# Two more Strassen products taken to a second level in the last down projection

## The chip, the cores and the metric

The kernel runs on one core of one Trainium2 chip. The metric is the device time of one execution, in microseconds (us). Five engines run their own instruction streams: TensorE (PE) multiplies and PEld loads its stationary operand, VectorE (DVE), ScalarE (ACT) and GpSimd (POOL) work on tiles, and SyncE (SP) issues nearly all transfers. Intermediate sums of the matrix products lie in eight PSUM banks; everything else lies in on-chip tiles or in memory.

## The reference

The reference is a linear-attention block followed by a gated feed-forward block, both with a layer norm in front and a residual added behind, on 2048 tokens of width 1024, with an inner width of 3584:

```python
def _B_ref(x, W_gate, W_up, W_down):
    gate = jnp.einsum("bsd,df->bsf", x, W_gate)
    up = jnp.einsum("bsd,df->bsf", x, W_up)
    gate = gate * (gate > 0)
    h = gate * up
    return jnp.einsum("bsf,fd->bsd", h, W_down)

h = x + _A_ref(_layernorm(x), A_wqkv, A_wo)
h2 = h + _B_ref(_layernorm(h), B_W_gate, B_W_up, B_W_down)
```

All inputs are bfloat16. The change touches the feed-forward block alone.

## The kernel before

The tokens of the feed-forward block are done in two passes of 1024. Each pass has a gate/up part of 14 *pairs* (two blocks of 128 inner columns a pair, `strassen_pair`, L1316) and a down part (`down_pass`, L1420). The attention block runs ahead of the first pass.

The order of work is written out by hand. Python builds one list of operations per engine (`_Plan`, L45 to 130). Each engine runs its list strictly in order, and waits are derived from which buffers an operation reads and writes. So the place in the program decides what is queued behind a waiting operation. This holds for SyncE too, whose list holds the transfers.

**Down part.** The output of a pass has 1024 tokens by 1024 columns. It is cut into 2 x 2 blocks of 512 tokens by 512 columns, and computed with Strassen's seven products (Winograd's form), numbered 0 to 6 in order of time. For each product the activations (or sums of them: D1 to D4) are multiplied by a block of W_down or by a sum of blocks (`t_scr`, made in the first gate/up pass by `wd_sums`, L650, and stored in memory). Products alternate between banks 0 to 3 (`XB`) and 4 to 7 (`YB`).

- A *direct* product (`direct`, L1547) has 56 matmuls of 512 columns, and takes its weights in five chunks (`WCH`).
- A *second-level* product (`level2`, L1575) applies the same scheme once more inside the product. It has seven steps, M1, M7, M6, M2, M5, M4 and M3 in this order, each of 14 matmuls of 256 columns with one weight chunk of 448 KB. The steps share four banks. ScalarE copies a bank to the next twice (`dfk`), and VectorE adds a bank into its target after M7 (two adds), M2, M5, M4 and M3. Step M3 accumulates into the bank that the add after M5 reads, so M3 waits for that add.

Before the change, products 1, 3, 5 and 6 are second-level and 0, 2 and 4 direct, in both passes. Each second-level product needs four sums of activations (`l2_sums`, L1509: VectorE, 1792 elements per partition, both operands in on-chip memory) and four sums of weights (`wl_sums`, L666, made in the first gate/up pass and stored in `l_scr`).

The products end in sums with each other and with the residual tiles: `U` starts as a copy of product 0, `V` is U plus product 3, and so on. The residual of the block (token half, column half) is fetched from `h_scr` in four tiles (`ld_h`, L1424) into a ring of eight slots, and GpSimd adds it to U or V (`add_h`, L1476), or makes the output of block (1,1) from `dsum` (`p_22`, L1469). VectorE makes the other outputs. `at(product, unit, ...)` hangs operations behind a unit of the list: a step of a second-level product, or a chunk of a direct one. Outputs are issued when `st_flush` is reached.

**Weight chunks.** `load_wd_next` (L612) issues the next chunk in order, each time a chunk was used, into the slot that came free. The first pass has a ring of 7 slots and the second of 13, of which six are gate/up weight slots (`RWG`) that the last three pairs leave:

```python
X_AT = [(NPAIR - 3) * 2 + i for i in range(NWX)]
RING = [[NWS - 2, NWS - 1] + list(range(NWS - 2))]
RING.append([RING[0][(len(WLIST) + i) % NWS] for i in range(NWS)] +
            [NWS + (NPAIR * 2 + x) % NWG for x in X_AT])
```

In the profile, L718 is every matmul, L723 every ScalarE copy, L543 every transfer and L1434 every sum of the down part: these are lines of helpers, so groups are told apart by tiles (`ps` is PSUM).

Of the kernel before, what the change touches and what calls it, by code (L numbers as in the profile page):

```python
# [132 lines left out]
def bass_sequential_preLN__linear_attn_block__glu_gated_reglu__prompt_kernel(  # L133
# [66 lines left out]
    l_scr = nc.dram_tensor("l_scr", [(len(L2O) + 1) * 4 * P, WDW], f16).ap()  # L200
# [5 lines left out]
    with es:  # L206
# [16 lines left out]
        NWX = 6  # L223
# [37 lines left out]
        hnT = RH[:].rearrange("p (a b) -> p a b", a=NDC)  # L261

# [42 lines left out]
        wdring += [RWG[:, i * NDC * 2 * P:i * NDC * 2 * P + WDW] for i in range(NWG)]  # L305
# [44 lines left out]
        def bank(b, w=512):  # L350
            return ps[:, b, 0:w]
# [22 lines left out]
        sl_lw = slots("dlw_", 2)  # L374
        sl_out = slots("dout_", NOS)
# [56 lines left out]
        B_out2 = bufs("out2_", STB)  # L432
        B_wd = bufs("wd_", NWS + NWX)
# [50 lines left out]
        for i in range(NWX):  # L484
            B_wd[NWS + i].over = [B_w[i]]
# [108 lines left out]
        WSRC = [("b", 0, 0), ("l", 1), ("b", 1, 0), ("l", 2), ("t", 0), ("l", 3), ("l", 4)]  # L594
        LSRC = [("q", 0, 0), ("s", 2), ("s", 1), ("q", 1, 0), ("s", 0), ("s", 3), ("q", 1, 1)]
        WLIST = []
        for src in WSRC:
            if src[0] == "l":
                WLIST += [("l", src[1]) + x for x in LSRC]
            else:  # L600
                WLIST += [src + c for c in WCH]

        X_AT = [(NPAIR - 3) * 2 + i for i in range(NWX)]
        RING = [[NWS - 2, NWS - 1] + list(range(NWS - 2))]
        RING.append([RING[0][(len(WLIST) + i) % NWS] for i in range(NWS)] +
                    [NWS + (NPAIR * 2 + x) % NWG for x in X_AT])

        def wd_slot(L):
            r = RING[L // len(WLIST)]
            return r[L % len(WLIST) % len(r)]  # L610

        def load_wd_next():  # L612
            L = wd_next[0]
            if L >= NPASS * len(WLIST):
                return
            wd_next[0] += 1
            i = wd_slot(L)
            src = WLIST[L % len(WLIST)]
            dst = wdring[i]
            if src[0] != "b":  # L620
                dst = dst.bitcast(f16)
            if src[0] == "l":
                dst = dst[:, 0:WDW].rearrange("p (m c) -> p m c", c=HNW)
                o = src[1]
                if src[2] == "q" and o == 4:
                    k, h = src[3:]
                    dma(sl_wd[i], wdring[i].rearrange("p (m c) -> p m c", c=HNW),
                        wd_v[:, 1, k:NPAIR:2, NW + h * HNW:NW + (h + 1) * HNW], "ld_wr_%d" % L, writes=[B_wd[i]])
                elif src[2] == "q":
                    k, h = src[3:]  # L630
                    dma(sl_wd[i], dst, t_v[:, o, k:NPAIR:2, h * HNW:(h + 1) * HNW], "ld_wq_%d" % L, reads=B_tscr,
                        writes=[B_wd[i]])
                else:
                    dma(sl_wd[i], dst, l_v[:, o - 1, src[3]], "ld_wl_%d" % L, reads=B_wscr if o == 4 else B_lscr,
                        writes=[B_wd[i]])
                return
            q0, q1 = src[-2:]
            dst = dst[:, 0:(q1 - q0) * NW].rearrange("p (q c) -> p q c", c=NW)
            if src[0] == "b":
                dma(sl_wd[i], dst, wd_v[:, src[1], q0:q1, src[2] * NW:(src[2] + 1) * NW], "ld_wd_%d" % L,  # L640
                    writes=[B_wd[i]])
            else:
                dma(sl_wd[i], dst, t_v[:, src[1], q0:q1, :], "ld_wt_%d" % L, reads=B_tscr[q0:q1],
                    writes=[B_wd[i]])
# [763 lines left out]
        os_ctr = [0]  # L1408
        wd_use = [0]
        U_ = [ftmp[:, j, :] for j in range(STB)]  # L1410
        V_ = [ftmp[:, STB + j, :] for j in range(STB)]

# [4 lines left out]
        X0v = hh16[:, 0:NFT:2, 0:SBW]  # L1417
        X1v = hh16[:, 0:NFT:2, SBW:2 * SBW]

        def down_pass(ps_, fill):  # L1420
            XB, YB = [0, 1, 2, 3], [4, 5, 6, 7]
            hr = {}

# [25 lines left out]
            def put(blk, dh, j, in0, in1, reads, eng="dve"):  # L1449
                k = os_ctr[0] % NOS  # L1450
                os_ctr[0] += 1
                tt(outst[:, k, :], in0, in1, reads, [B_outst[k]], "out_%d_%d_%d" % (blk, j, dh), eng=eng)
                st_out(blk, dh, j, sl_out[k], outst[:, k, :], B_outst[k])
# [5 lines left out]
            def e_s1(j):  # L1459
                ident_act(U_[j], bank(XB[j]), [B_bank[XB[j]]], [B_U[j]], "ds1")  # L1460

# [4 lines left out]
            def e_22(j):  # L1466
                tt(dsum[:, j, :], bank(XB[j]), V_[j], [B_bank[XB[j]], B_V[j]], [B_dsum[j]], "d22")

            def p_22(j):  # L1469
                h, hb = hv(1, 1, j)  # L1470
                put(1, 1, j, dsum[:, j, :], h, [B_dsum[j], hb], "pool")

            def e_u5(j):
                tt(U_[j], bank(XB[j]), U_[j], [B_bank[XB[j]]], [B_U[j]], "dU5")

            def add_h(dst, bufs_, blk, dh, j):  # L1476
                h, hb = hv(blk, dh, j)
                tt(dst[j], dst[j], h, [hb], [bufs_[j]], "dh", eng="pool")

            def quad(base, T, H):  # L1480
                return ftmp[:, base + 2 * T:base + 2 * T + 2, H * HNW:(H + 1) * HNW]
# [4 lines left out]
            def l2_add(dst, bd, src, bs, T, H, b, name):  # L1486
                tt(quad(dst, T, H), qb(b), quad(src, T, H), [B_bank[b]] + ([] if src == dst else bs[2 * T:2 * T + 2]),
                   bd[2 * T:2 * T + 2], name)

            def l2_out(ost, bo, base, bs, T, H, b):  # L1490
                tt(ost[:, 2 * T:2 * T + 2, H * HNW:(H + 1) * HNW], qb(b), quad(base, T, H),
                   [B_bank[b]] + bs[2 * T:2 * T + 2], bo[2 * T:2 * T + 2], "out_%d%d" % (T, H))

            def a_hh(k, t, f=hh):
                return (lambda q, j: f[:, 2 * q + k, (t * STB + j) * P:(t * STB + j + 1) * P]), \
                       (lambda q: B_hh[2 * q + k][t])
# [4 lines left out]
            def d2(q):  # L1501
                tt(D2[:, q, :], D1[:, q, :], hh[:, 2 * q, 0:SBW], [B_D1[q], B_hh[2 * q][0]], [B_D2],
                   "D2_%d" % q, op=ALU.subtract)

            def d4(q):
                tt(hh16[:, 2 * q + 1, 0:SBW], hh[:, 2 * q + 1, 0:SBW], D2[:, q, :], [B_D2],
                   [B_hh[2 * q + 1][0]], "D4_%d" % q, op=ALU.subtract)

            def l2_sums(quarter, dst, name):  # L1509
                def go(j, x, y, op):  # L1510
                    d, bd = dst(j)
                    tt(d, x[0], y[0], x[1] + y[1], bd, "%s_%d" % (name, j), op=op)
                Q = quarter
                return [
                    lambda: go(2, Q(0, 0), Q(0, 1), ALU.subtract),
                    lambda: go(0, Q(0, 1), Q(1, 1), ALU.add),
                    lambda: go(1, dst(0), Q(0, 0), ALU.subtract),
                    lambda: go(3, Q(1, 0), dst(1), ALU.subtract),
                ]

            def q_d2(k, t):
                return D2[:, k:NPAIR:2, t * SHB:(t + 1) * SHB], [B_D2]

            def q_hh(par, f):
                def go(k, t):
                    i0 = 2 * k + par
                    return f[:, i0:NFT:4, SBW + t * SHB:SBW + (t + 1) * SHB], [B_hh[i][1] for i in range(i0, NFT, 4)]
                return go

            def sg_ro(j):  # L1530
                return sg_o[:, j], [B_sgo[j]]

            def sg_x0(j):
                b0, c0 = NM * (j // 2), (j % 2) * SHB
                return X0v[:, b0:b0 + NM, c0:c0 + SHB], [B_hh[2 * (b0 + m)][0] for m in range(NM)]

            def sg_x1(j):
                b0, c0 = NM * (j // 2), (j % 2) * SHB
                return X1v[:, b0:b0 + NM, c0:c0 + SHB], [B_hh[2 * (b0 + m)][1] for m in range(NM)]

            def q_d4(k, t):
                i0 = 2 * k + 1
                return hh16[:, i0:NFT:4, t * SHB:(t + 1) * SHB], [B_hh[i][0] for i in range(i0, NFT, 4)]
# [3 lines left out]
            def direct(pi, bk, act_ops, w16, start, evac):  # L1547
                af, ab = act_ops
                for ci, (q0, q1) in enumerate(WCH):
                    def go(ci=ci, q0=q0, q1=q1):  # L1550
# [3 lines left out]
                        if w16:  # L1554
                            w = w.bitcast(f16)
# [19 lines left out]
            def level2(pi, bks, Q, sg, evac):  # L1575
                a, f, b, c = bks

                def prod(mi, bk, x, start):
                    xa, xb = x
                    ws = wd_slot(wd_use[0])  # L1580
                    wd_use[0] += 1
                    w = wdring[ws]
                    if pi != 6 or mi in (5, 6, 7, 4):
                        w = w.bitcast(f16)
# [40 lines left out]
            def ev(dst, bd, src, bs, name):  # L1625
                def go(m, b):
                    if m == 2:
# [388 lines left out]
```

## Time and profile before

| | |
|---|---|
| median of 4 runs | 733.77 us (733.12 to 734.61) |
| the profiled execution | 734.54 us, its span 732.8 us |
| second gate/up pass | from 480.2 us |
| last down pass | products 0 to 6 from 649.4 us to the end |
| VectorE busy, 500 to 550 us (second gate/up pass) | 33.6 of 50 us |
| GpSimd busy, 500 to 690 us | 0 |

The span runs from the first to the last instruction. The page of the profile gives each engine's busy time and its share of the span. The chain that ended last is followed back from the last instruction, at each step to what released it. A timeline lists instructions in order of time, merged where several follow each other on one engine with the same operands; "x14" is their number, and the bracket at the end is the engine's idle time ahead and what ended it. Only time on the engine that sets the end counts.

### The profile page before, as it was taken

Reading aid. Unit: us, or ns where it says so; the run is one execution under the profiler, and the core shown is the slowest. Engines: PE = TensorE matmul, PEld = TensorE weight load, DVE = VectorE, ACT = ScalarE, POOL = GpSimd, SP = SyncE. Lnnn points to the kernel's source line nnn. Section 1 sums busy time; section 2 is a strip of 40 time slices with the busy share of each in tenths; the row PEclk is TensorE's granted clock in tenths of the full one; section 3 lists DMA queues with packets and bytes.
Section 4 is the critical chain, followed back from the end, with each engine's and each line's share of the span. In section 5 each row is a group of like instructions: output and inputs, shape, how many; then the busy total and the mean of one; then the engine's idle time right before and its main releaser. Section 6 shows DMA issues by size and latency. Waiting matters only on the chain.

```text
span 732.8 us, 11571 instructions
## 1 busy us (share of the span) xinstructions
PE 723.2 (99%) x4311; PEld 363.5 (50%) x4311; DVE 553.9 (76%) x976; ACT 352.8 (48%) x614; POOL 104.7 (14%) x169
## 2 busy tenths in 40 slices
PE   8999999999999999999999999999999999999997
PEld 3444444344444444444444666854444444447766
DVE  7878867898776988898888769765757575676593
ACT  4878667764832456777754100134445454521000
POOL 1311100000450103231311003500000000000052
PEclk9999999999999999999999999999999999999999
DMA  9642244024999797789887999994424242337892
GB/s 311 206 112 62 38 134 155 6 30 67 220 227 258 213 282 205 239 260 305 244 249 223 315 246 329 324 318 128 115 58 114 59 116 59 100 103 248 241 307 87
DMA packets 191880, 133.93 MB, mean 183 GB/s; under 512 B 51664, under 2 KB 173776, under 8 KB 191824
## 3 DMA queue, kind: packets, MB, share of 16 engines
q1 hardware_dynamic: 191152, 132.54, 63.9%
q8 instruction: 34, 0.56, 0.3%
q10 hardware_dynamic: 672, 0.66, 0.3%
q14 instruction: 22, 0.18, 0.1%
HBM read 96.47 MB, written 25.17 MB: 166 GB/s over the span
## 4 chain that ended last, share of the span: by engine, by line
PE 84%; DVE 8%; DMA 2%; issue 2%; ACT 2%; SPq 1%; POOL 1%; POOLq 0%; DVEq 0%; ACTq 0%
PE ps L718 84%; DVE RAB L1434 2%; DMA RAB<-in_A_wqkv_dram 1%; DVE RAB L804 1%; DVE RE L1179 1%; DVE RX L801 1%; DMA RE<-RE 1%; ACT RX L797 1%; DVE RX L1020 1%; DVE RW L914 1%; SPq L543 1%; POOL RE L1434 0%; DVE RC L914 0%; DVE RO L1434 0%; DVE RXH L1203 0%
## 5 line engine op out<-in xcount | busy, mean ns | idle before, releaser
L723 ACT ACTIVATE ps<-ps 128x512 f32<-128x512 f32 x172 | 100.1, 582 | 213.3 <-PE ps L718 153.7
L718 PE MATMUL ps<-RC,RO 128*128 128x512 f16 x672 | 154.2, 379 | 0.0
L718 PE MATMUL ps<-RH,RWG 128*128 128x512 bf16 x448 | 105.8, 379 | 0.0
L718 PEld LDWEIGHTS ps<-RC,RO 128*128 128x128 f16 x672 | 65.8, 98 | 79.3
L1353 DVE TENSOR_TENSOR RAB<-ps,RAB 128x512 bf16<-128x512 f32 x56 | 38.6, 689 | 74.2 <-PE ps L718 74.2
L718 PE MATMUL ps<-RC,RWG 128*128 128x512 f16 x320 | 76.8, 379 | 0.3 <-ACT ps L723 0.3
L1349 DVE TENSOR_TENSOR RE<-ps,RE 128x512 bf16<-128x512 f32 x112 | 74.4, 685 | 1.6 <-PE ps L718 0.7
L718 PEld LDWEIGHTS ps<-RH,RWG 128*128 128x128 bf16 x448 | 43.8, 98 | 52.6
L1434 POOL TENSOR_TENSOR RE<-RE,RX 128x512 f32<-128x512 f32 x16 | 23.6, 1505 | 288.2 <-DMA RX<-h_scr 284.2
L723 ACT ACTIVATE RE<-RE 128x512 bf16<-128x512 bf16 x56 | 35.1, 627 | 60.6 <-DVE RE L1349 59.9
L718 PE MATMUL ps<-RW,RAB 128*128 128x256 f16 (+3 forms) x404 | 62.9, 313 | 0.0
L718 PE MATMUL ps<-RH,RO 128*128 128x512 bf16 (+1 forms) x256 | 61.2, 379 | 0.0
L718 PE MATMUL ps<-RW,RE 128*128 128x512 bf16 x256 | 57.6, 379 | 0.9 <-DVE RXH L1203 0.7
L723 ACT ACTIVATE RE<-ps 128x512 f32<-128x512 f32 x64 | 37.7, 597 | 35.8 <-PE ps L718 35.8
L718 PE MATMUL ps<-RAB 128*128 128x512 bf16 (+1 forms) x258 | 54.3, 350 | 0.1
L718 PEld LDWEIGHTS ps<-RW,RAB 128*128 128x128 f16 (+1 forms) x404 | 39.5, 98 | 21.2
L718 PEld LDWEIGHTS ps<-RC,RWG 128*128 128x128 bf16 (+1 forms) x320 | 30.0, 98 | 40.2 <-ACT ps L723 6.2
L1297 DVE TENSOR_TENSOR RO<-RWG 128x1024 f16<-128x1024 bf16 x54 | 36.9, 684 | 8.0 <-DMA RWG<-in_B_W_up_dram 8.0
L723 ACT ACTIVATE RAB<-ps 128x512 bf16<-128x512 f32 x56 | 33.4, 597 | 15.8 <-PE ps L718 14.6
L1434 DVE TENSOR_TENSOR RE<-ps,RE 128x512 f32<-128x512 f32 x40 | 27.0, 687 | 18.2 <-PE ps L718 15.4
L718 PEld LDWEIGHTS ps<-RH,RO 128*128 128x128 f16 (+1 forms) x256 | 24.4, 98 | 30.1 <-ACT RX L723 1.6
L718 PEld LDWEIGHTS ps<-RW,RE 128*128 128x128 bf16 x256 | 24.0, 98 | 28.9 <-DVE RXH L1203 1.2
(140 smaller groups left out, 1002.4 us busy)
## 6 DMA issues: line engine op xcount, KB each, us to landing
RWG<-in_B_W_gate_dram SPq DMA_DIRECT2D x28, 512.0 KB, 5.4
RWG<-in_B_W_up_dram SPq DMA_DIRECT2D x28, 512.0 KB, 6.2
RW<-in_B_W_down_dram SPq DMA_DIRECT2D x14, 512.0 KB, 5.4
t_scr<-RW SPq DMA_DIRECT2D x14, 512.0 KB, 4.1
RE<-in_A_x_dram SPq DMA_DIRECT2D x23, 256.0 KB, 3.8
RW<-l_scr SPq DMA_DIRECT2D x13, 448.0 KB, 4.8
l_scr<-RX SPq DMA_DIRECT2D x7, 768.0 KB, 8.6
h_scr<-RXH SPq DMA_DIRECT2D x16, 256.0 KB, 3.3
```

What stands on the lines that cost most here:

```text
L543: return PL.add(eng, lambda e: e.dma_start(dst_ap, src_ap), reads=reads, writes=writes, slot=slot, name=name)
L718: lambda e: e.matmul(out_ap, lhsT, rhs, start=start, stop=stop, skip_group_check=skip),
L723: PL.add("act", lambda e: e.activation(out=dst, in_=src, func=func), reads=reads, writes=writes, name=name)
L797: PL.add("act", lambda e: e.activation(out=Et[:, k, :], in_=src, func=ACTF.Exp), reads=[src_buf], writes=[B_E[k]], name=name + "_exp")
L801: PL.add("dve", lambda e: e.tensor_scalar(out=Et[:, k, :], in0=Et[:, k, :], scalar1=1.0, scalar2=1e-6, op0=ALU.min, op1=ALU.add), reads=[] ...
L804: PL.add("dve", lambda e: e.scalar_tensor_tensor(out=dst_ap, in0=src, scalar=C1, in1=Et[:, k, :], op0=ALU.add, op1=ALU.max), reads=[src_bu ...
L914: PL.add("dve", lambda e: e.tensor_tensor(out=t(j)(d), in0=in0(d), in1=in1(d), op=ALU.subtract), reads=reads, writes=[btw[j]], name="%s%d" ...
L1020: PL.add("dve", lambda e: e.tensor_tensor(out=s_, in0=p_, in1=s_, op=ALU.add), reads=[pb], writes=[sb_], name=name + "_add")
L1297: PL.add(eng, lambda e: e.tensor_tensor(out=tb(j, u), in0=f0(u), in1=f1(u), op=ALU.subtract), reads=[B_w[i + x] for x in r] + ([B_T[k + x] ...
L1349: PL.add("dve", lambda e: e.tensor_tensor(out=dst, in0=src, in1=ftmp[:, w, :], op=ALU.add), reads=[bsrc, B_s5[w]], writes=[bdst], name=name)
L1353: PL.add("dve", lambda e: e.tensor_tensor(out=dst, in0=a_, in1=b_, op=ALU.mult), reads=reads, writes=[wr], name=name)
L1434: PL.add(eng, lambda e: e.tensor_tensor(out=dst, in0=in0, in1=in1, op=op), reads=reads, writes=writes, name=name)
```

## The change

In the second pass, products 2 and 4 become second-level too, so that six of the seven are. The first pass keeps its four.

- Products 2 and 4 need weight sums that no one makes yet. In pairs 1 to 7 of the second gate/up pass VectorE makes them (`x_wsums`): eight sums of 256 elements a pair, from 512 KB fetched by SyncE (`load_xr`) ahead, stored 512 KB a pair to `l_scr`. The tiles used lie in `RW`, where four weight slots of the down part are. So the prefetch of the down weights, issued at the end of the first down pass before, waits until after pair 8.
- The last pass has 9 weight slots in place of 13. Four of the six slots taken from `RWG` now hold the activation sums for products 2 and 5 (`sg_g`). The sums for product 2 are made in the last pair, but for a seventh.
- A second-level product adds bank by bank into its targets instead of leaving a sum in the banks. Product 2 is added to a copy `W` of product 0, which ScalarE makes (`e_w`) and to which GpSimd adds the residual of block (0,0) during product 1. Product 4 is added into two targets, `dsum` (with V) and U, so it has twice the adds.
- VectorE's sums for products 4, 5 and 6 lie in products 2, 3 and 5; before, those for 5 and 6 lay in product 4. The D4 sums lie at the start of products 3 and 5. In both passes D2 and D4 are made in two operations of 7 x 512 elements each, not in 14 of 512.
- The residual tiles of a block are fetched sooner: (0,1) at product 2 and not 3 in the first pass; in the last pass (0,0) at product 0, (0,1) at 1, (1,1) at 2, (1,0) at 4. GpSimd's adds to U and V and its outputs of (1,1) move with them.

```diff
-        NWX = 6
+        NWX = 2
...
+        L2SET = [(1, 3, 5, 6), (1, 2, 3, 4, 5, 6)]
...
+        RING = [[NWS - 2, NWS - 1] + list(range(NWS - 2)),
+                [NWS - 2, NWS - 1, NWS - 3] + list(range(NWS - 3)) + [NWS + i for i in range(NWX)]]
...
+        def load_xr(m):
+            if m < NM:
+                z = m % 2
+                dma(sl_xr[z], xr[:, z, 0].bitcast(f16), t_v[:, 0, 2 * m:2 * m + 2, :], "ld_xr_%d" % m,
+                    reads=B_tscr[2 * m:2 * m + 2], writes=[B_xr[z][0]])
+                dma(sl_xw[z], xr[:, z, 1], wd_v[:, 1, 2 * m:2 * m + 2, 0:NW], "ld_xw_%d" % m, writes=[B_xr[z][1]])
+
+        def x_wsums(m):
...
+                add(0, q_(0, 1), q_(0, 0))
+                add(2, q_(1, 1), q_(0, 1))
+                add(1, q_(1, 1), t_(0))
+                add(3, q_(1, 0), t_(1))
+
+            def fin():
+                dma(sl_lx[z], l_v[:, 4:6, :, m, :].rearrange("p o j c -> p (o j) c"),
+                    lx[:, z].rearrange("p s j c -> p (s j) c"), "st_lx_%d" % m, reads=flat(B_lx[z]),
+                    writes=[B_xscr[m]])
+                load_xr(m + 2)
+            return [lambda: one(0), lambda: one(1), fin]
...
+            def d4(a, b):
+                tt(hh16[:, 2 * a + 1:2 * b:2, 0:SBW], hh[:, 2 * a + 1:2 * b:2, 0:SBW], D2[:, a:b, :], [B_D2],
+                   [B_hh[2 * q + 1][0] for q in range(a, b)], "D4", op=ALU.subtract)
...
-            direct(2, XB, a_hh(1, 0), False, False, e_11)
...
-            direct(4, XB, a_d1(), True, True, e_22)
...
+            if last:
+                level2(2, XB, q_10, sgs[2], ev_out(0, 0, WV, OS, sl_out))
+            else:
+                direct(2, XB, a_hh(1, 0), False, e_11)
+            level2(3, YB, q_d3, sgs[3], ev("dV", (V, U)))
+            if last:
+                level2(4, XB, q_d1, sgs[4], ev("d5", (DS, V), (U, U)))
+            else:
+                direct(4, XB, a_d1(), True, e_22)
...
+            if not last:
...
+                at(2, 3, lambda: ld_h(0, 1))
...
+            else:
...
+                at(0, 0, lambda: ld_h(0, 0))
+                at(0, 3, *l2_sums(q_10, sg_rg, "sg2", NM - 1, NM))
+                at(1, 0, *each(e_w), *each(add_h, WV, 0, 0))
+                at(1, 3, lambda: ld_h(0, 1))
+                at(2, 0, lambda: ld_h(1, 1))
+                for i in range(4):
+                    at(2, 2 + i, sg5[i])
+                    at(3, 2 + i, sg4[i])
+                    at(5, 1 + i, sg3[i])
+                at(3, 0, lambda: d4(0, NH))
+                at(3, 6, *each(add_h, U, 0, 1, order=hi))
+                at(5, 0, lambda: d4(NH, NPAIR))
+                at(4, 1, lambda: ld_h(1, 0))
+                at(4, 3, *each(add_h, V, 1, 0, order=(2, 3)))
+                at(4, 6, *each(add_h, V, 1, 0, order=(0, 1)))
+                at(5, 0, *each(p_22, order=hi))
...
+                else:
+                    if q == 0:
+                        claim(flat(B_xr) + flat(B_lx), B_wd[0:NWS - 3])
+                        load_xr(0)
+                        load_xr(1)
+                    if 1 <= q <= NM:
+                        w0_, w1_, wf_ = x_wsums(q - 1)
+                        mid[0].append(w0_)
+                        mid[1] += [w1_, wf_]
...
+                if p_ == 1 and q == NM + 1:
+                    claim(B_wd[0:NWS - 3], flat(B_xr) + flat(B_lx))
+                    wd_lim[0] = len(WLIST)
+                    for _ in range(NWS):
+                        load_wd_next()
+                if p_ == 1 and q == NPAIR - 1:
+                    for i in range(NWX):
+                        claim([B_wd[NWS + i]], [B_w[i]])
+                        load_wd_next()
...
-                if p_ == 1 and q >= NPAIR - 3:
-                    load_wd_next()
-                    load_wd_next()
```

## The prediction

> **What bounds the kernel now.** I read the head of the page first (which engine is full), then the chain that ended last (where it leaves TensorE), then the timeline of the last down pass for the price of each piece, and last the transfers of that stretch. In the page:
>
> ```profile
> span 732.8 us, 11571 instructions
> PE 723.2 (99%) x4311; PEld 363.5 (50%) x4311; DVE 553.9 (76%) x976; ACT 352.8 (48%) x614; POOL 104.7 (14%) x169
> ...
> PEclk9999999999999999999999999999999999999999
> ```
>
> TensorE is the bound, at full clock, so a change pays what it takes off TensorE's work or idle time. The chain shows how little idle time there is in the second half:
>
> ```profile
> 205.26 261.70 PE ps L718 x1440
> 467.00 0.20 issue
> 467.20 0.69 DVE RAB L1434
> 467.89 0.05 issue
> 467.94 227.20 PE ps L718 x1204
> ...
> 716.25 0.69 DVE RAB L1434
> 716.95 0.05 issue
> 716.99 12.41 PE ps L718 x112
> 729.43 0.69 DVE RX L1434
> ```
>
> From 205 us to the end it leaves TensorE at two places, both in product 5 of a down pass, before step M3; then comes a tail of some 3 us that the change leaves alone. The timeline of the last down pass gives the prices:
>
> ```profile
> 661.47 1.69 PE L718 MATMUL ps<-RAB,RC 128*128 128x256 f16 x14
> 663.00 1.69 PE L718 MATMUL ps<-RE,RO 128*128 128x256 f16 x14
> ...
> 672.17 2.75 PE L718 MATMUL ps<-RWG,RAB 128*128 128x512 bf16 x12
> ...
> 694.96 5.34 PE L718 MATMUL ps<-RWG,RXH 128*128 128x512 f16 x24
> ...
> 699.80 7.20 POOL L1434 TENSOR_TENSOR RE<-RE,RX 128x512 f32<-128x512 f32 x4 [228.79 <-DMA RX<-h_scr]
> ...
> 707.04 3.22 PE L718 MATMUL ps<-RW,RAB 128*128 128x256 f16 x28
> 707.87 2.47 DVE L1434 TENSOR_TENSOR RO<-ps,RE 128x512 f32<-128x512 f32 x4
> ...
> 710.95 4.50 POOL L1434 TENSOR_TENSOR RE<-RE,RX 128x512 f32<-128x512 f32 x4 [3.95 <-DVE RE L1434]
> ```
>
> A second-level step (14 matmuls of 256 columns) takes 663.00 - 661.47 = 1.53 us, so product 1, seven steps, takes 672.17 - 661.47 = 10.70 us. The direct product 4 takes 707.04 - 694.96 = 12.08 us. Product 5 starts at 707.04, so its seventh step M3 was due at 716.21; it came at 716.99, 0.78 us late. In the first down pass product 5 starts at 457.61, M3 was due at 466.77 and came at 467.94: 1.17 us late.
>
> The same timeline, cut finer, shows two engines taking turns:
>
> ```profile
> 695.76 3.21 DVE L1434 TENSOR_TENSOR RAB<-RAB 128x1792 f16<-128x1792 bf16 x3
> ...
> 700.02 4.00 DVE L1434 TENSOR_TENSOR RAB<-RAB 128x1792 f16<-128x1792 f16 x2
> ```
>
> A 1792-element VectorE sum of two SBUF operands takes 1.07 us alone and 2.00 us while GpSimd adds run; the adds go from 1.12 us (4.50 for four) to 1.8 and more. A pair takes as long as one after the other, so a GpSimd add holds such a sum up by up to 0.95 us. VectorE's adds out of PSUM keep 0.62 us (2.47 for four) beside GpSimd work. Last, 690 to 710 us, where the transfer engines are full:
>
> ```profile
> DMA packets 6677, 6.32 MB, mean 316 GB/s; under 512 B 396, under 2 KB 6011, under 8 KB 6675
> ...
> RX<-h_scr SPq DMA_DIRECT2D x12, 128.0 KB, 5.8
> ```
>
> **The matmuls.** Two direct products become second-level ones: 2 x (12.08 - 10.70) = 2.8 us less TensorE work, all on the path. *Taken: -2.8.* The Trainium skill speaks against it: its page "TensorE: Matmul & The Clock Gate", section "Back-to-back issue gap", gives streams of load-and-multiply pairs as about 81 ns a matmul at 128 columns and 131 at 512. By that the direct product would take 56 x 0.131 = 7.3 us, the other, at some 98 ns between, 9.6 us, and the change would cost about 4.6 us. The rows here are 216 ns for 512 columns (12.08/56) and 109 for 256 (10.70/98), and they decide.
>
> **The weight sums in the second gate/up pass.** Eight VectorE sums of 256 elements per pair, in seven pairs. A 512-element sum takes 0.42 us and one of 1792 takes 1.08, so 256 elements take about 0.29: 2.3 us a pair. VectorE is busy 33.6 of 50 us there (500 to 550) (8.1 a pair of 12.1 us); with 2.3 it is 86% busy, as in the first gate/up pass (85.5 of 100 us between 300 and 400), where TensorE is 100.0 busy. Its transfers, 1 MB a pair beside 1 MB of gate/up weights, are 174 GB/s against 316. The weight prefetch that SyncE issued around 480 us moves to the ninth pair. *Taken: 0*; if the cover were gone, 2.3 us a pair would show.
>
> **First down pass.** D2 and D4 go from 14 sums each to two of 3584 elements (2.0 us by the same slope, 4.0 instead of 6): beside matmuls, 0. The residual tiles of (0,1) are fetched at product 2 instead of 3. GpSimd's adds to U, which started at 451.17 when those tiles came, can start at 446.4, when VectorE has read U; this frees the slots for (1,0) sooner and takes 1.9 us of issues out of SyncE's queue around 445 us. That fetch was issued at 457.59 behind a transpose that took SyncE 4.61 us, and the adds to V started at 462.06; their lateness is the 1.17 us at M3. If everything behind 447 moves up, all of it goes; if the transpose's issue still sets the time, about 0.3. *Taken: -0.8* (0 to -1.17); next to bind would be VectorE's evacuation of M5, due 0.1 us ahead of M3.
>
> **Last down pass, products 1 to 4.** Times are from the start of each product. M3 waits for the evacuation of M5, which is due at 7.9; M3 at 9.17. In product 1, GpSimd now adds residual tiles to the new copy W (four adds from 2.9) beside VectorE's sums: an evacuation at 8.1 to 8.75 is just in time, *0* (0 to 0.65). ScalarE's four copies, 2.1 us, fit the 2.48 us that it waited there. Product 2 has the pattern of today's product 1: 0. In product 3, two adds to U meet two sums: VectorE runs evacuations to 4.65, sum to 5.7, add to 6.65, evacuation to 7.0, add to 7.65, sum to 8.7, evacuation to 9.38; M3 is *0.3* late (0 to 0.7). In product 4 every evacuation is doubled: two after M5, 7.92 to 9.23, *0.05*.
>
> **Last down pass, product 5.** Here VectorE's D4 half (2.0) and the sums for product 6 meet GpSimd's adds to V and the four outputs of (1,1); today those sums are over by 708 and meet only the adds to U. Residual tiles (1,0) are issued at 3.1 to 5.1 of product 4 and land 5.8 us later, at 10.9; adds to V from there, to 13.1 = 2.4 of product 5. VectorE: last evacuations of product 4 to 1.5; D4 half waits for an add and runs 2.2 to 4.2; two evacuations of M7 to 5.5; GpSimd has adds to 6.2; sum to 7.25; output add to 8.2; sum to 9.25; evacuation to 9.9; output add to 10.2; sum to 11.25; evacuation of M5 to 11.9. M3 starts at 12.0 instead of 9.17: 2.8 us late, 0.78 today. *Taken: +2.0.* Bounds: with no turns taken the same list ends at 9.4 (0.3 late: -0.5); with all four two-operand operations held 0.95 each, at 13.2 (4.1 late: +3.3). I take the middle value since the adds are there when three of the four arrive.
>
> **Transfers.** From product 1 to the last weight issue, 50 us, SyncE asks for 34 weight loads of 0.459 MB and 16 tiles of 0.131 MB: 17.7 MB, 350 GB/s against 316, so 1.8 MB or 5.6 us of delay gathers. With nine slots a load is due 12.2 us after its issue and lands some 5 to 7 us after it today: *0*, with some 5 us to spare before it is more.
>
> **The sum:** -2.8 - 0.8 + 0.3 + 0.05 + 2.0 = -1.2 us. The profiled execution took 734.54 us for its span of 732.8; the median is 733.77, 0.77 lower. 733.77 - 1.2 = 732.6 us.
>
> **Rivals.** *The turns cost little:* were the GpSimd work over before VectorE's sums, product 5 would be 0.3 late and product 3 on time: -2.8 - 0.8 - 0.5 = -4.1 us, 729.7. For it: GpSimd needs only 6.7 us for its six adds. Against it: the adds to V's upper half wait for the last evacuation of product 4. *The residual tiles come late (slower):* the fetch for (1,0) stands behind weights in a full queue. If they land x us into product 4, x above 14, the adds follow D4, and M3 of product 5 is late by x - 9.8. All other terms sum to -4.0 (the 0.78 of today included), so slower by 0.2% needs 5.5 us, x = 15.3: a landing 10 us after issue, against 5.8 in the row and 6.9 for the slowest (692.95 to 699.80). It needs transfers at some 285 GB/s. At x = 16.5 the time would be 736.4. *TensorE's clock falls in the gap:* no idle gap between 205 us and the tail reaches 1.2 us, and the granted clock shows no loss there; in the tail, 730 to 733 us, it is 0.86. By the row it costs nothing. The same page, section "Why this matters for your kernels", warns of idle gaps over about 3 us, after which the clock is halved; by it a gap of 3.4 us would cost some 1.7 us of estimate more.
>
> **How the numbers follow.** 0.2%, 1.5 us, is about what a measurement of this kernel can tell from no change. My sum: 0.55, spread over -2.5 to +1, so part of it is faster by more than that. The turns cost little: 0.27, faster. Late tiles or a longer gap: 0.18, mostly slower. Faster 0.46, same 0.36, slower 0.18. Best bounds together (-2.8, -1.17, -0.5) give 729.3, worst (+3.3, +0.65, +0.7 - 2.8) 735.6; cutting a tenth at each end gives 730.0 to 735.3.
>
> **What would show it.** Right: products 2 and 4 of the last pass each 10.7 us; in product 5 a gap of 2 to 3 us before M3, released by VectorE, with VectorE sums of about 2 us beside GpSimd; M3 of the first pass's product 5 less than 0.9 late; no TensorE wait for a weight load. Wrong: a gap under 1 us in product 5 (the turns were overpriced), TensorE waiting for weights (nine slots too few), or GpSimd waiting long for residual tiles in product 4.

## The result, and the profile after

The changed kernel takes 735.46 us (median of 51 runs, 733.14 to 737.91), the kernel before 733.80 in the runs beside them (72 runs, 732.78 to 736.67). The ratio is 1.0019, with a 95% interval of 1.0013 to 1.0025: 0.2% slower, 1.4 us by the ratio and 1.7 us between the medians, where 1.2 us less was predicted. The profiled execution took 737.21 us for a span of 735.4, so it is one of the longer ones; before it was 734.54 for 732.8.

The head of the page of the changed kernel:

```profile
span 735.4 us, 11822 instructions
PE 722.7 (98%) x4395; PEld 372.4 (51%) x4395; DVE 571.7 (78%) x1002; ACT 356.8 (49%) x622; POOL 116.2 (16%) x173
...
PEclk9999999999999999999999999999999999999999
```

84 matmuls more, and TensorE is busy 0.5 us less: something has taken the 2.8 us back. The 40 slices do not show it, because each is 18 us long. The end of the chain does (start, length, what; matmuls are now L765, the VectorE and GpSimd additions L1523, the sums of activations L1463):

```profile
468.01 221.22 PE ps L765 x1204
...
692.35 12.44 PE ps L765 x112
...
717.92 14.08 PE ps L765 x112
732.02 0.69 DVE RX L1523
```

The chain leaves TensorE for M3 of product 3 (692.35) and of product 5 (717.92). The last row holds 112 matmuls: M3 of product 5 and product 6. The row of before with the same 112 matmuls took 12.41 us. So two things are new: M3 of product 5 comes later, and the work behind it takes 1.67 us longer. For the second, look at the granted clock. Of the changed kernel, stretches of 2 us with the busy time (and count) of PE, PEld, DVE, ACT and POOL, the granted clock, the share of the transfer engines and GB/s:

```profile
716.00:718.00 2.00, 0.08 (x1) 0.09 (x2) 2.00 (x3) 0.00 (x0) 2.00 (x2) 1.00 1.00 345
718.00:720.00 2.00, 2.00 (x14) 1.56 (x15) 1.82 (x2) 0.00 (x0) 2.00 (x2) 0.72 0.60 197
720.00:722.00 2.00, 2.00 (x12) 1.43 (x10) 0.69 (x1) 0.00 (x0) 0.23 (x1) 0.50 0.40 135
722.00:724.00 2.00, 2.00 (x19) 1.73 (x18) 0.00 (x0) 0.58 (x1) 0.00 (x0) 0.93 0.60 200
```

The clock falls about a microsecond after TensorE starts again, to half, and is back some 3.4 us later: 2 x (0.28 + 0.50 + 0.07) = 1.7 us are lost. Before M3, the timeline (start, length, engine, line, operation, count, idle time ahead and its releaser):

```profile
706.02 2.02 DVE L1523 TENSOR_TENSOR RAB<-RAB,RC 128x3584 f16<-128x3584 bf16 x1
706.12 6.26 POOL L1523 TENSOR_TENSOR RE<-RE,RX 128x512 f32<-128x512 f32 x4 [8.29 <-DVE RE L1523]
...
710.20 1.42 DVE L1523 TENSOR_TENSOR RE<-ps,RE 128x512 f32<-128x512 f32 x2 [2.16 <-POOL RE L1523]
711.53 3.77 DVE L1463 TENSOR_TENSOR RAB<-RAB 128x1792 f16<-128x1792 f16 x2
712.36 7.88 POOL L1523 TENSOR_TENSOR RX<-RH,RX 128x512 bf16<-128x512 f32 x4
...
717.92 2.30 PE L765 MATMUL ps<-RW,RWG 128*128 128x256 f16 x14 [3.97 <-DVE RAB L1523]
720.01 5.86 PE L765 MATMUL ps<-RW,RAB 128*128 128x256 bf16 x42
```

Read it downwards. VectorE's half of D4 starts 0.1 us ahead of GpSimd's first add to V, and that add, 1.12 us alone, takes 2.93. The second ends at 710.17, and until then VectorE can't evacuate M7 into the same V: it stands idle for 2.16 us. After that each of its sums (L1463) runs beside one of GpSimd's four outputs of (1,1), and a pair of sums takes 3.77 us instead of 2.1. Product 5 started at 704.62, so M3 was due at 713.78. It came 4.14 us late, and TensorE waited 3.97 us by its row.

In the profiled execution the sum, measured, is: two products -2.8, first down pass -0.1, product 3 +0.25, product 5 4.14 - 0.78 = +3.4, clock +1.7: +2.5, against +2.6 in the span.

**The clock over all runs.** Each run records the mean granted clock of its span. A fall like the one above shows as 0.997 or 0.998. Of the 51 runs of the changed kernel 34 have such a value, and four have 0.995, which is what two such falls would give. The median of these 38 is 735.69; the other 13, at 1.000, have a median of 733.81. None of the runs of before for which the clock was recorded beside the experiments (62) is below 0.999. So without the fall the changed kernel is as fast as the one before, and with it 1.9 us slower.

### The profile page after: what moved, and what is told of

Read it like the earlier page. It is cut to its first block, busy times and chain, and to the rows that moved or that the text cites. A ratio compares the mean times of both kernels' runs of the same rounds, so it can differ in the third digit from the quotient of the medians.

```text
span 735.4 us, 11822 instructions
## 1 busy us (share of the span) xinstructions
PE 722.7 (98%) x4395; PEld 372.4 (51%) x4395; DVE 571.7 (78%) x1002; ACT 356.8 (49%) x622; POOL 116.2 (16%) x173
## 4 chain that ended last, share of the span: by engine, by line
PE 84%; DVE 6%; DMA 3%; ACT 3%; SPq 2%; issue 2%; POOL 1%; POOLq 0%; DVEq 0%; ACTq 0%
PE ps L765 84%; DMA RE<-in_A_x_dram 2%; DMA RW<-t_scr 1%; DVE RAB L851 1%; ACT RX L844 1%; SPq L556 1%; DVE RE L1226 1%; SPq L560 1%; ACT RXH L803 1%; DVE RX L848 1%; DVE RAB L1463 1%; POOL RE L1523 1%; ACT ps L770 1%; DMA RX<-h_scr 0%; DVE RE L1523 0%
## 5 line engine op out<-in xcount | busy, mean ns | idle before, releaser
L770 ACT ACTIVATE ps<-ps 128x512 f32<-128x512 f32 x176 | 102.5, 582 | 212.0 <-PE ps L765 209.8
L765 PE MATMUL ps<-RC,RO 128*128 128x512 f16 x672 | 154.2, 379 | 0.0
L765 PEld LDWEIGHTS ps<-RC,RO 128*128 128x128 f16 x672 | 65.7, 98 | 79.3
L765 PE MATMUL ps<-RH,RWG 128*128 128x512 bf16 x448 | 105.8, 379 | 0.0
L765 PE MATMUL ps<-RC,RWG 128*128 128x512 f16 x320 | 76.9, 379 | 0.7 <-ACT ps L770 0.6
L765 PEld LDWEIGHTS ps<-RH,RWG 128*128 128x128 bf16 x448 | 43.9, 98 | 52.6
L765 PE MATMUL ps<-RH,RO 128*128 128x512 bf16 (+1 forms) x256 | 61.2, 379 | 0.0
L765 PE MATMUL ps<-RW,RE 128*128 128x512 bf16 x256 | 57.6, 379 | 1.5 <-DVE rden L1224 0.8
L765 PE MATMUL ps<-RW,RAB 128*128 128x256 f16 (+3 forms) x404 | 58.4, 302 | 0.0
L765 PE MATMUL ps<-RAB 128*128 128x512 bf16 (+1 forms) x270 | 57.0, 351 | 0.1
L765 PEld LDWEIGHTS ps<-RC,RWG 128*128 128x128 bf16 (+1 forms) x320 | 30.0, 98 | 40.6 <-ACT ps L770 6.7
L765 PEld LDWEIGHTS ps<-RW,RAB 128*128 128x128 f16 (+1 forms) x404 | 40.1, 99 | 15.5
L1523 DVE TENSOR_TENSOR RE<-ps,RE 128x512 f32<-128x512 f32 x42 | 28.6, 687 | 18.0 <-PE ps L765 11.9
L765 PEld LDWEIGHTS ps<-RH,RO 128*128 128x128 f16 (+1 forms) x256 | 24.4, 98 | 30.1 <-ACT RX L770 1.6
L765 PEld LDWEIGHTS ps<-RW,RE 128*128 128x128 bf16 x256 | 24.0, 98 | 29.5 <-DVE RXH L1250 1.2
L765 PEld LDWEIGHTS ps<-RAB 128*128 128x128 bf16 (+1 forms) x270 | 26.0, 98 | 24.3 <-ACT RAB L911 1.0
```

Source lines behind the costliest of these rows:

```text
L765: lambda e: e.matmul(out_ap, lhsT, rhs, start=start, stop=stop, skip_group_check=skip),
L770: PL.add("act", lambda e: e.activation(out=dst, in_=src, func=func), reads=reads, writes=writes, name=name)
L1523: PL.add(eng, lambda e: e.tensor_tensor(out=dst, in0=in0, in1=in1, op=op), reads=reads, writes=writes, name=name)
```

## The experiments

The theory, after this reading, has two parts. *Place:* GpSimd's adds and outputs in product 5 meet VectorE's work, and hold up M3 by 4.1 us. *Clock:* the idle gap this leaves is long enough to halve the clock in most runs. The first rival is that product 5 is late from something else (its second-level evacuations, or the transfers); the second, that the longer product 6 comes from its own operands and not from the gap. A third question was what the first down pass gives by itself.

Each experiment stands against runs of the kernel before that were taken beside it, so their median differs (733.50 to 734.07). The ratio with its interval compares the runs, not the two medians, and can differ from the medians' quotient by about 0.001. M3 is due six steps after the start of its product; "late" is counted from there.

**1. The tiles sooner.** The residual tiles of (1,0), which the adds to V need, change places with those of (1,1). Times of all fetches stay.

```diff
-                at(2, 0, lambda: ld_h(1, 1))
+                at(2, 0, lambda: ld_h(1, 0))
...
-                at(4, 1, lambda: ld_h(1, 0))
+                at(4, 1, lambda: ld_h(1, 1))
```

> In the last pass the residual tiles of (1,0) are fetched at product 2 and those of (1,1) at product 4, the other way round than in the changed kernel. Theory 'turns' (GpSimd's adds to V and outputs of (1,1) take turns with VectorE's D4 half and sums): the two adds to V's upper half are over before product 5, the other GpSimd work stays, so M3 of product 5 is 2.3 to 3.0 us late in place of 4.1; that gap is under the length after which the clock fell, so product 6 takes 10.7 us again, and the median is 732.0 to 732.8. Theory 'tiles' (only the late landing of (1,0) makes the gap): M3 less than 0.5 late, 730 to 731. Theory 'transfers' (the full transfer queue with nine weight slots): no change, 735.5.

Measured: 732.96 us (12 runs) against 734.07, ratio 0.9988 (0.9975 to 1.0001). In its timeline:

```profile
704.55 4.05 POOL L1523 TENSOR_TENSOR RE<-RE,RX 128x512 f32<-128x512 f32 x2 [4.60 <-DVE RH L1523]
704.99 2.60 DVE L1523 TENSOR_TENSOR RAB<-RAB,RC 128x3584 f16<-128x3584 bf16 x1
708.57 7.03 POOL L1523 TENSOR_TENSOR RX<-RH,RX 128x512 bf16<-128x512 f32 x4
708.83 3.79 DVE L1463 TENSOR_TENSOR RAB<-RAB 128x1792 f16<-128x1792 f16 x2
...
715.25 1.70 PE L765 MATMUL ps<-RW,RWG 128*128 128x256 f16 x14 [2.33 <-DVE RAB L1523]
```

Only two of the four adds are left for product 5, and they take the turn ahead of D4. M3, due at 712.74, is 2.51 us late instead of 4.14, in the range expected; the median is 0.2 us above the expected one. The sums (3.79 for two) still meet the outputs. The clock holds in this execution, but it fell in 5 of the 12 runs (median 734.49; the other seven 732.79), which the expectation did not allow for.

**2. The outputs held back.** Instead of the swap, GpSimd's four outputs of (1,1) wait for VectorE's evacuation of M5, so that they can't run beside the sums ahead of it. The helpers `put` and `tt` only pass the new dependence on.

```diff
-                put(1, 1, j, DS[0][:, j, :], h, [DS[1][j], hb], "pool")
+                put(1, 1, j, DS[0][:, j, :], h, [DS[1][j], hb], "pool",
+                    deps=[PL.prog["dve"][-1]] if last else ())
...
+                at(5, 4, *each(p_22, order=hi))
...
-                at(5, 0, *each(p_22, order=hi))
```

> The changed kernel, but GpSimd's four outputs of (1,1) wait for VectorE's evacuation of M5 in product 5, so they meet none of the sums ahead of it. 'Turns': the two sums that took 2.0 us beside outputs take 1.1, M3 of product 5 is 2.7 to 3.3 late in place of 4.1, which is near the length at which the clock falls: 732.5 to 734.5. 'Tiles' and 'transfers': M3 still about 4 late, 735.5.

Measured: 734.07 us (12 runs) against 734.07, ratio 0.9993 (0.9982 to 1.0004). Its timeline, and one of its stretches of 2 us:

```profile
705.25 2.02 DVE L1523 TENSOR_TENSOR RAB<-RAB,RC 128x3584 f16<-128x3584 bf16 x1
705.50 6.11 POOL L1523 TENSOR_TENSOR RE<-RE,RX 128x512 f32<-128x512 f32 x4 [8.44 <-DMA RX<-h_scr]
709.43 1.42 DVE L1523 TENSOR_TENSOR RE<-ps,RE 128x512 f32<-128x512 f32 x2 [2.16 <-POOL RE L1523]
...
715.83 2.81 PE L765 MATMUL ps<-RW,RWG 128*128 128x256 f16 x14 [2.65 <-DVE RAB L1523]
```

```profile
716.00:718.00 2.00, 2.00 (x13) 1.45 (x11) 1.37 (x2) 0.00 (x0) 2.00 (x2) 0.56 0.59 189
```

Here the releaser of the adds is named as the transfer of the tiles (`h_scr`), and D4 is again ahead of them by 0.25 us: VectorE's wait of 2.16 us at M7 is that of the changed kernel to the hundredth. The outputs no longer run beside the last two sums, and M3, due at 713.01, is 2.82 us late. So the swap takes 1.6 us off M3's lateness and the hold 1.3; the two together make 2.9 of the 4.14 us. The clock fell in the profiled execution after a gap of only 2.65 us, and in 5 of 12 runs.

**3. The gap filled.** The changed kernel, with 14 matmuls of 512 columns on old data, into banks that no one reads any more, ahead of M3 of product 5. M3 still waits for the same addition; TensorE is only kept busy meanwhile.

```diff
                 def m3():
+                    if last and pi == 5:
+                        for i in range(14):
+                            mm(bank(XB[i % 2]), D2[:, 0, 0:P], D2[:, 1, :], True, True, [B_D2], B_bank[XB[i % 2]],
+                               "fill", skip=True)
                     prod(3, c, sg(3), False)
```

> The changed kernel with 14 matmuls of 512 columns (3.0 us) put ahead of M3 of product 5, into banks that no one uses then. They leave the result as it is and only keep TensorE busy in the gap. 'Clock' (the 1.7 us that product 6 lost is the granted clock falling after a gap of over 3.4 us): M3 comes as late as before, at about 4.1, but the granted clock stays at 1.00 and product 6 takes 10.7 us; the median falls from 735.5 to 733.6 to 734.0. Rival (product 6 is slow because its weights or the port are late): product 6 still takes 12.4 us and the median stays 735.5 or rises.

Measured: 734.10 us (12 runs) against 734.07, ratio 1.0001 (0.9991 to 1.0010), and the clock at 0.999 or more in all 12 runs. In its timeline:

```profile
704.16 6.28 POOL L1523 TENSOR_TENSOR RE<-RE,RX 128x512 f32<-128x512 f32 x4 [7.97 <-DMA RX<-h_scr]
704.38 2.81 DVE L1523 TENSOR_TENSOR RAB<-RAB,RC 128x3584 f16<-128x3584 bf16 x1
...
712.15 3.19 PE L765 MATMUL ps<-RC 128*128 128x512 f16 x14
715.97 1.70 PE L765 MATMUL ps<-RW,RWG 128*128 128x256 f16 x14 [0.64 <-DVE RAB L1523]
717.51 4.75 PE L765 MATMUL ps<-RW,RAB 128*128 128x256 bf16 x42
```

M3 is nearly as late as before (3.82 us), yet the 42 matmuls of product 6 that took 5.86 us take 4.75. So the idle gap, and not product 6, costs the rest: 1.0019 becomes 1.0001, 1.3 us. The first two rows show something else: here GpSimd's first add starts 0.22 us ahead of D4, not behind it, and M3 is only 0.3 us less late.

**4. Both, with the sums spread.** Swap and hold together, and the four sums for product 6 behind steps M7, M6, M5 and M4 of product 5 instead of M7, M6, M2 and M5.

```diff
-                    at(5, 1 + i, sg3[i])
+                    at(5, (1, 2, 4, 5)[i], sg3[i])
```

> The swap of the fetches and the wait of the outputs of (1,1) together, and of VectorE's four sums for product 6 the third stands behind the evacuation of M5. 'Turns': one add meets the D4 half, nothing meets the two sums; M3 of product 5 is 0 to 0.5 late, the clock stays, and the time is 733.8 - 2.8 (matmuls) - 0.5 (M3) - 0.6 (first pass) + 0.3 (product 3) = 730.2, 729.8 to 731.0. If something else than the GpSimd work and the place of that sum holds M3 up, the gap stays over 1.5 us and the time over 731.5.

Measured: 730.34 us (6 runs) against 734.07, ratio 0.9943 (0.9929 to 0.9958). In its timeline:

```profile
703.89 4.05 POOL L1523 TENSOR_TENSOR RE<-RE,RX 128x512 f32<-128x512 f32 x2 [4.60 <-DVE RH L1523]
704.32 2.60 DVE L1523 TENSOR_TENSOR RAB<-RAB,RC 128x3584 f16<-128x3584 bf16 x1
...
708.17 2.08 DVE L1463 TENSOR_TENSOR RAB<-RAB 128x1792 f16<-128x1792 f16 x2
...
711.64 6.07 POOL L1523 TENSOR_TENSOR RX<-RH,RX 128x512 bf16<-128x512 f32 x4 [3.69 <-issue]
712.09 1.69 PE L765 MATMUL ps<-RW,RWG 128*128 128x256 f16 x14
```

The two sums take 2.08 us, M3 starts without a wait, and the clock was at 0.999 or more in all 6 runs. The four outputs run behind the evacuation of M5. Swap and hold had taken off 2.9 of the 4.14 us; that the spread of the sums gives the remaining 1.2 is a difference, not a measurement, as no run has the spread alone.

**5. No GpSimd work in product 5.** The adds to V and the four outputs of (1,1) are left out of the last pass, everything else is as in the changed kernel.

```diff
-                at(4, 3, *each(add_h, V, 1, 0, order=(2, 3)))
-                at(4, 6, *each(add_h, V, 1, 0, order=(0, 1)))
-                at(5, 0, *each(p_22, order=hi))
```

> The changed kernel without any GpSimd work in product 5 of the last pass: the residual is left out of block (1,0) and block (1,1) is not written in the last pass. 'Turns': VectorE's list runs through undisturbed, M3 of product 5 is 0.2 to 0.6 late, the clock stays, 733.8 - 2.8 - 0.5 + 0.3 - 0.6 = 730.2 (729.8 to 731.0). If VectorE's own load (D4 half, three sums, the doubled evacuations of product 4) makes the gap, M3 stays over 1.5 late.

Measured: 730.13 us (6 runs) against 733.53, ratio 0.9943 (0.9929 to 0.9958). Its timeline:

```profile
704.47 2.02 DVE L1523 TENSOR_TENSOR RAB<-RAB,RC 128x3584 f16<-128x3584 bf16 x1
706.40 1.41 DVE L1523 TENSOR_TENSOR RE<-ps,RE 128x512 f32<-128x512 f32 x2
707.73 2.08 DVE L1463 TENSOR_TENSOR RAB<-RAB 128x1792 f16<-128x1792 f16 x2
...
712.24 1.69 PE L765 MATMUL ps<-RW,RWG 128*128 128x256 f16 x14
```

Without GpSimd's eight operations VectorE's list fits, in its old order, and M3 is on time. That is the whole loss of product 5, and experiment 4 gets the same time with the operations in place. It rules out the first rival: with the same evacuations, and the same fetches of tiles and weights, M3 is not late.

**6. Only product 2.** Product 4 stays direct; the order around it is that of the kernel before.

```diff
-        L2SET = [(1, 3, 5, 6), (1, 2, 3, 4, 5, 6)]
+        L2SET = [(1, 3, 5, 6), (1, 2, 3, 5, 6)]
...
-            if last:
-                level2(4, XB, q_d1, sgs[4], ev("d5", (DS, V), (U, U)))
-            else:
-                direct(4, XB, a_d1(), True, e_22)
+            direct(4, XB, a_d1(), True, e_22)
...
-                at(5, 0, lambda: d4(NH, NPAIR))
+                at(4, 0, lambda: d4(NH, NPAIR))
+                for i in range(4):
+                    at(4, i, sg3[i])
...
+                at(5, 0, *each(add_h, V, 1, 0, order=hi), *each(p_22), *each(e_u5))
```

> One part of the change alone: in the last pass product 2 is second-level, product 4 direct as before, and the D4 half and the sums for product 6 lie beside product 4 again; GpSimd's adds to V begin when product 4 is read. 'Turns': half of the matmul gain, and no operation of VectorE with two operands in on-chip memory is left in product 5, so M3 there is 0 to 0.4 late: -1.4 - 0.6 (M3) - 0.6 (first pass) + 0.3 = -2.3, 731.5 (731.0 to 732.2). If the nine slots or the transfers are at fault, they are so here too and M3 or a weight load is late by over 1 us.

Measured: 731.57 us (6 runs) against 733.53, ratio 0.9962 (0.9949 to 0.9976), with no wait of TensorE from 400 us on. Half of the change alone beats the whole of it. The other half is worth the difference to experiment 4, 0.0019 or 1.4 us, with some 0.0014 of uncertainty on each ratio; the matmuls of one product give 12.08 - 10.70 = 1.4 us. It comes out only when product 5 is put in order for it.

**7. The first pass's fetch alone.** The kernel before, with only the tiles of (0,1) in the first down pass fetched at product 2.

```diff
-            at(3, 4, lambda: ld_h(0, 1))
+            at(*((2, 3) if ps_ == 0 else (3, 4)), lambda: ld_h(0, 1))
```

> The kernel before, with one part of the change alone: in the first pass the tiles of (0,1) are fetched at product 2 in place of 3. As the prediction has it: M3 of product 5 in the first pass is 0.1 to 0.9 late in place of 1.17, the time falls by 0.3 to 1.1 us, 733.2 against 733.9. Rival (the fetch of (1,0) is held by the transpose ahead of it in SyncE's queue): M3 still 1.2 late, no change.

Measured: 733.38 us (12 runs) against 733.53, ratio 1.0001 (0.9990 to 1.0012). The time misses what was expected. The trace does not: the steps M4 and M3 of product 5 in the first pass,

```profile
465.06 1.69 PE L718 MATMUL ps<-RAB 128*128 128x256 f16 x14
466.80 3.23 PE L718 MATMUL ps<-RE,RAB 128*128 128x256 f16 x28
```

start 1.74 us apart, so M3 is 0.2 us late instead of 1.17. From the first step of product 1 to the end of the pass that execution needed 67.45 us, and before 68.13. The interval of the ratio reaches from -0.7 to +0.9 us, so it does not show a gain; one of 0.7 us lies at its edge.

**8. Five matmuls in the gap.** Experiment 3 with `range(5)`, 1.2 us of filling, which leaves a shorter gap.

> The changed kernel with 5 matmuls of 512 columns (1.08 us) ahead of M3 of product 5. They shorten the idle stretch from about 4 to 2.7 to 3.0 us and leave M3 as late as it is. 'Clock': the clock falls in some executions and not in others, less often than in the changed kernel (38 of 51) and about as often as with the gaps of 2.3 to 2.7 us of the two single mends (11 of 24); the median is between 734.0 and 735.4.

Measured: 734.87 us (12 runs) against 733.50, ratio 1.0014 (1.0001 to 1.0027). In the profiled execution M3 is 4.14 us late and the clock holds:

```profile
712.77 1.24 PE L765 MATMUL ps<-RC 128*128 128x512 f16 x5
...
716.91 1.70 PE L765 MATMUL ps<-RW,RWG 128*128 128x256 f16 x14 [2.89 <-DVE RAB L1523]
718.45 4.75 PE L765 MATMUL ps<-RW,RAB 128*128 128x256 bf16 x42
```

But over the runs it fell in 8 of 12 (median 735.11; the other four 733.90). One profile would have said that 2.89 us of idle time are harmless; the runs say that they are not. The last section shows from the profiles why both happen.

**9. The version that beats both.** Experiment 4, with the sums for product 5 spread over product 3 in the same way and, in the first pass, the tiles of (1,0) fetched ahead of those of (1,1).

```diff
-                at(4, 0, lambda: ld_h(1, 1), *each(add_h, U, 0, 1))
-                at(4, 2, lambda: ld_h(1, 0))
+                at(4, 0, lambda: ld_h(1, 0), *each(add_h, U, 0, 1))
+                at(4, 2, lambda: ld_h(1, 1))
...
-                    at(3, 2 + i, sg4[i])
+                    at(3, (2, 4, 5, 6)[i], sg4[i])
```

> The kernel with both mends in product 5 and two more: in product 3 of the last pass VectorE's second sum stands behind the evacuation of M5 (M3 there was 0.25 late), and in the first pass the tiles of (1,0) are fetched before those of (1,1) (M3 of product 5 there was 0.58 late). 'Turns' and 'first pass: late tiles': both M3 on time, no wait of TensorE on VectorE left in either down pass, 0.8 us less than with the two mends alone: 729.5 (729.0 to 730.2). If the first pass's lateness comes from the adds' own length, its M3 stays 0.5 late and the time is 730.1.

Measured: 729.94 us (6 runs) against 733.53, ratio 0.9943 (0.9930 to 0.9956), as in experiment 4: the two extra edits show nothing in the time. The waits of TensorE from 400 us to the end, in all:

```profile
PE ps L765 <- DMA RE<-in_B_W_down_dram: 0.3, 1, 0.3
```

It is a weight load of the first pass. What the changed kernel was meant to save, and the 0.8 us that the kernel before lost in product 5, come out here.

## Why the prediction was wrong

The forecast was 732.6 us, 1.2 less than before, in a range of 730.0 to 735.3; the time is 735.46, 1.7 more. "Slower" had a chance of 0.18. Two terms failed: product 5 was taken at +2.0 us and cost 3.4, and the fall of the clock was taken at nothing and cost 1.7.

- **The matmuls** (-2.8): right. Products 2 and 4 of the last pass run from 672.25 to 682.95 and from 693.89 to 704.62, 10.70 and 10.73 us. The rows were right against the Trainium skill's streams of 81 and 131 ns ("TensorE: Matmul & The Clock Gate", "Back-to-back issue gap"), by which the change would have cost about 4.6 us.
- **The weight sums in the second gate/up pass** (0): right. That pass starts at 480.25 and the last down pass at 649.46; before, 480.17 and 649.38.
- **First down pass** (-0.8, 0 to -1.17): of the right size in the traces, but not in the profiled execution, where the pass took 68.01 us against 68.13: M3 of product 1 waited 0.28 us for a weight chunk (`t_scr`), and M3 of product 5 was still 0.58 us late. The seven executions of experiments 1 to 6 and 8, which have the same first pass, took 66.97 to 67.79. With the one above the median of eight is 67.40, -0.7 us. There is one execution of before to hold against them, and experiment 7 did not show it in the time, so this term stays unproven.
- **Products 1 to 4** (+0.3 and +0.05): right. M3 of product 3 is 0.25 late and that of product 4 0.04.
- **Transfers** (0): right. TensorE waits for no weight in the last pass. The slots were enough. The 316 GB/s taken as what the full transfer engines move was not their limit: the stretch from 697 to 707 us moved 352. What did come late are the residual tiles, in the next item.
- **Product 5** (+2.0, bounds -0.5 to +3.3): the mechanism was right, and the step that failed is the landing of the residual tiles (1,0). I had them issued at 3.1 to 5.1 us of product 4 and landing 5.8 us later, so that two adds to V would be over by 2.4 us of product 5. They were issued at 3.9 to 6.4, with a median of 6.7 us to landing, and the first add started at 12.2 us of product 4 instead of 10.9 (at 11.9, 12.4 and 12.9 in experiments 3, 2 and 8, where the row names the transfer as the releaser). Its row in the changed kernel names VectorE; but by the program this add needs of VectorE nothing later than the evacuation of M7 in product 4, long done, so there too it waited for its tile. With the adds that late, D4 (12.1) goes first, and the two evacuations of M7 in product 5, which wait for the second add, end at 7.0 us of product 5 instead of 5.5. From there the list ran nearly as predicted, and M3 was 4.14 us late instead of 2.8.

  The late tiles weigh more than who goes first. In experiment 3 the add was ahead of D4, as predicted, only 1.0 us later than predicted, and M3 was 3.82 us late. That D4 goes first adds at most 0.3. The rival "the residual tiles come late" is what happened, but its formula, x - 9.8 from x = 14 on, fits only in part: it gives 4.2 us at x = 14, and 4.14 was reached at 12.2 and again at 12.9 (experiment 8).

  Two smaller readings were off as well. The row at 707.87, read as VectorE beside GpSimd work, lies between two stretches of it; the next four additions, from 710.26 to 712.73, run beside the adds from 710.95 on and take the same 2.47 us. And not the adds to V's upper half but the other two wait for the last evacuation of product 4: in experiment 1 the upper ones are over before product 5.
- **TensorE's clock in the gap** (nothing): wrong, and the larger miss. I priced it by rows with gaps up to 1.2 us, which could say nothing about a gap three times as long, and with 2.8 us took the warning of the Trainium skill ("TensorE: Matmul & The Clock Gate", "Why this matters for your kernels": gaps over about 3 us) as not reached. The estimate from that page, 1.7 us for a 3.4 us gap, is what the runs show: 1.7 us in the profile, 1.9 between the two groups of runs. The limit of about 3 us does not agree with them: a gap of 2.65 us was enough in experiment 2. Even the gap of 2.8 us that I forecast should have been priced.

With these two terms put right, and the unproven -0.7 kept, -2.8 - 0.7 + 0.3 + 3.4 is +0.2 us for the runs without the fall, measured 0.0; with 1.7 for the fall it is +1.9, measured +1.9.

## What to carry to other kernels

When TensorE is the bound and work is taken off it, draw up the lists of the engines that feed it, step by step, for the stretch that got shorter: here 2.8 us of matmuls went, and VectorE and GpSimd had to put the same additions into less time beside more evacuations. Take the landing times of the tiles from the new order of transfers, not from the old. If the list shows a gap of more than about 2 us, price the clock behind it too, and decide between two orders that differ by a few tenths by moving a fetch or a sum, not by hoping. A change that measures as nothing or slightly slower can hold its whole gain in the order of the work around it: three small edits of the order made 1.0019 into 0.9943.

## What the runs showed of the hardware

The clock does not fall at a sharp limit of the gap. Each row gives the idle time ahead of M3 of product 5 in the profiled execution, and the runs in which the mean clock was below 0.999:

| Kernel | idle, us | runs with the fall | median with, without, us |
|---|---|---|---|
| experiment 3 | 0.64 | 0 of 12 | -, 734.10 |
| experiment 1 | 2.33 | 5 of 12 | 734.49, 732.79 |
| experiment 2 | 2.65 | 5 of 12 | 734.83, 733.10 |
| experiment 8 | 2.89 | 8 of 12 | 735.11, 733.90 |
| the changed kernel | 3.97 | 38 of 51 | 735.69, 733.81 |

The same kernel has runs with and without it, so what a gap of this length costs is a chance times some 1.2 to 1.9 us. The gap of each single run is not recorded: a fall can belong to a longer gap than the one in the profile.

What decides can be read from the profiles. In all eleven profiled executions the granted clock changes only on a grid of 3.413 us, whatever the program does then; relative to the first instruction the grid lies differently in each execution (the first change to full clock comes 4.8 to 7.2 us after it). Three executions, cut along their own grid (the columns are those of the 2 us stretches above; the first after the comma is TensorE's busy time):

```profile
715.45:718.87 3.42, 0.95 (x9) 0.86 (x10) 3.42 (x4) 0.00 (x0) 3.42 (x3) 1.00 0.91 312
718.87:722.28 3.41, 3.41 (x18) 2.44 (x17) 1.64 (x3) 0.00 (x0) 1.36 (x1) 0.50 0.49 167
...
712.83:716.24 3.41, 0.76 (x8) 0.45 (x6) 3.41 (x5) 0.00 (x0) 0.34 (x1) 1.00 1.01 348
716.24:719.65 3.41, 3.41 (x18) 2.44 (x17) 1.82 (x3) 0.00 (x0) 3.41 (x3) 0.50 0.43 139
...
712.40:715.81 3.41, 1.62 (x10) 0.72 (x8) 3.41 (x3) 0.00 (x0) 3.41 (x3) 1.00 1.00 340
715.81:719.22 3.41, 2.31 (x22) 2.08 (x23) 3.41 (x5) 0.00 (x0) 3.41 (x2) 1.00 0.84 272
```

They are the changed kernel, experiment 2 and experiment 8. In the changed kernel 2.47 of the 3.97 us of idle time fall into one stretch of the grid, in experiment 2 all 2.65; the next stretch has half the clock. In experiment 8 the 2.89 us are cut into 1.79 and 1.10 (in experiment 1 the 2.33 into 0.81 and 1.53), and the clock stays. In the eleven executions together, tails included, every stretch at full clock that was followed by one at half had TensorE busy for at most 1.24 us, and every other one for at least 1.62 us. So it is not the length of the gap that counts but how much of it one stretch gets, and the limit lies somewhere between 1.8 and 2.2 us of idle time in 3.41. The kernel does not choose where the grid lies, so a gap somewhat longer than that costs by chance, and each fall costs half of one stretch, 1.7 us.

Which engine gets to go first is settled by tenths of a microsecond, and the other one pays. D4 ahead by 0.1 us makes the GpSimd add take 2.93 us instead of 1.12; the add ahead by 0.44 us (experiment 1) makes D4 take 2.60 instead of 2.02. For M3 the turn itself made at most 0.3 us (experiment 3).
